# Gated products taken one block at a time instead of two joined, with a new order of all steps

## The chip, the cores and the metric

One core of one Trainium2 chip runs the whole program. The metric is the device time of one execution in microseconds. The engines that matter are TensorE (PE in the profile, its weight loads PEld), VectorE (DVE), ScalarE (ACT), GpSimd (POOL) and SyncE (SP), which here only issues transfers. Each engine takes its instructions strictly in the order in which the program lists them, so a step that waits holds everything behind it on the same engine.

## What is computed

The input `A_u` is 2048 tokens of 512 channels in bf16. It is normalized per token, and the output is the sum of the input, a long convolution and a gated layer:

```python
x = A_u
xn = _layernorm(x, axis=-1)
# A: per channel d a kernel K[d, l] = Re sum_n C * exp(dt*A*l) * dt*B, convolved causally
#    over 2048 tokens (by FFT in the reference), plus xn * Dskip
# B:
g = jnp.einsum("bsd,df->bsf", xn, w_gate)     # 512 -> 1792
u = jnp.einsum("bsd,df->bsf", xn, w_up)
h = _sigmoid(g) * u
b = jnp.einsum("bsf,fd->bsd", h, w_down)      # 1792 -> 512
return x + A(xn) + b
```

## The kernel before

**The planner.** The kernel first builds a list of steps (`pl.add`), which are numbered in the order in which they are added, each with an engine and a function that emits one or a few instructions. A hand-kept list `ORDER` of these numbers then says in which order the functions are called, and so the order of each engine's queue. Slots of buffers are handed out and given back along this list. Steps 0 to 605 are the normalization and the convolution, the steps from 606 on the gated layer; the numbers up to 605 mean the same in both kernels.

**The head.** Four loads bring tokens 0 to 511, one a part of the parameters (`l_pa`, three 128x512 blocks). TensorE first runs matmuls on zeros (`keep_warm`, L519). Tokens are normalized in pairs of tiles: VectorE and ScalarE take statistics (L542, L534), GpSimd a power (L492), VectorE scales (L554), TensorE transposes (L565), and the result goes to `xnT`: the first pair by step 35 on ScalarE (L572), the second by step 46 on VectorE (L574). Only then can the first gate matmuls run, for blocks 6 to 9 in halves (`HALF`): the first 256 tokens need step 35, the others step 46. Beside this the first parameters are worked up: step 47 an exponential on ScalarE (L608, waits for `l_pa`), steps 48 and 49 products on VectorE (L610), step 50 on ScalarE (L615, waits for 48), step 51 on VectorE (L618, L619, waits for 50), step 52 an exponential on ScalarE (L621, waits for 49).

**The convolution.** VectorE builds power tables for four chunks of 128 channels (`PCH`, chunks 0 to 3) by complex products (L736, L737, L741, L742) and squares (L795, L796, squares on ScalarE at L790), after a ladder of squarings (L669, L676, L678). When a chunk's tables are done, TensorE multiplies them (L821), ScalarE copies the result up (`kq_sb`), SyncE stores it to DRAM and loads it back transposed after every second chunk, and VectorE adds one row (L842). The last table step of chunk 3 is number 364. Then, for two halves of the channels (p = 0, 1) and eight units u each: forward transform (L883), copy up, a swap of half rows (by four transfers, or by four copies on VectorE, L896), kernel transform (L909), two products on VectorE (L914, L918), inverse transform (L933), copy up, store. p = 1 can start its L909 only after L842 of the second pair of chunks.

**The gated layer.** Tokens go in four groups of 512 (`grp`), the hidden dimension in 14 blocks of 128 (`k`), of which two neighbours make a pair `u2` that shares a slot of `hT_sb`. Per block: four gate matmuls (L1043), a sigmoid on ScalarE from PSUM into `hT_sb` (L1055, or L1058 for two blocks at once in four pairs of `JOINT`), four up matmuls (L1067), and the gated product on VectorE. For blocks in `UEV` ScalarE copies the up product from PSUM to `us_sb` first (L1082), and gives the PSUM bank back; these products are made for both blocks of a pair at once (L1087, 1024 columns). `us_sb` has two slots of two blocks. For the others VectorE reads PSUM (L1092, 512 columns). After all 14 blocks follow four down products of 14 matmuls (L1121), a copy to `glu_sb` and, for groups 0 to 2, transfers from the GpSimd queue that add the input (L1158). The last sums (L1018, L1141) and the stores end the program.

**GpSimd's other part.** For tokens 512 on, in groups of four tiles, GpSimd makes the step between statistics and scaling (L481, L482); VectorE's L501 and L502 (one step, numbers 102, 119 and 136 for the three groups) wait for it.

Of the kernel before, what the change touches and what calls it, by code (L numbers as in the profile page):

```python
# [10 lines left out]
BF = mybir.dt.bfloat16  # L11
F32 = mybir.dt.float32
I32 = mybir.dt.int32
ACT = mybir.ActivationFunctionType
ALU = mybir.AluOpType
# [10 lines left out]
FT = 14  # L26
# [21 lines left out]
FLIP = ((0, 3), (0, 5), (1, 0), (1, 1), (1, 2), (1, 4), (1, 5), (1, 6), (2, 0), (2, 4), (3, 2))  # L48
JOINT = ((0, 2), (0, 3), (0, 5), (0, 6))
PF1 = 58.63  # L50
PSIG = 18.15
# [4 lines left out]
PPROD = 23.23  # L56
# [126 lines left out]
def _consts():  # L183
# [19 lines left out]
UEV = (6, 7, 10, 11, 12, 13, 14, 15, 16, 17, 18, 19, 22, 23, 24, 25, 26, 27, 28, 29, 30, 31, 32, 33, 34, 35, 36, 37, 38, 39, 40, 41, 44, 45, 46, 47, 52, 53, 54, 55,)  # L203
# [115 lines left out]
def kernel(  # L319
# [25 lines left out]
    def bank(slot, r=0):  # L345
        if slot.pool == "s":
            return pairs[slot.idx][:, 512 * r:512 * r + 512]
        return banks[slot.idx][:]
# [17 lines left out]
    us_sb = const.tile([128, 2, 2, 512], BF, name="us_sb")  # L366
# [381 lines left out]
    for c in range(4):  # L748
# [11 lines left out]
        n = 1  # L760
# [262 lines left out]
    for grp in range(4):  # L1023
# [5 lines left out]
        for u2 in range(7):  # L1029
# [4 lines left out]
            for k in (2 * u2, 2 * u2 + 1):  # L1034
# [38 lines left out]
                un = FT * grp + k  # L1073
                on = un in UEV

                if on:
                    if k % 2 == 0:
                        eu0, es0 = (b, mu, k), es_
                        continue
                    eus, us = [], _Slot("us")  # L1080
                    for n, (sl, m_, kk) in enumerate([(b, mu, k), eu0] if (grp, u2) in FLIP else [eu0, (b, mu, k)]):
                        eus.append(pl.add("ACT", 0.48, lambda sl=sl, us=us, kk=kk: S.activation(out=us_sb[:, us.idx, kk % 2, :], in_=bank(sl), func=ACT.Identity),  # L1082
                                          [m_] + eus, PSIG, acq=[] if n else [us], rel=[sl], alt=(FT * grp + kk, 1)))

                    def fpd2(hs=hs, us=us):
                        hh = hT_sb[:, hs.idx, :, :].rearrange("p k n -> p (k n)")
                        V.tensor_tensor(out=hh, in0=hh, in1=us_sb[:, us.idx, :, :].rearrange("p k n -> p (k n)"), op=ALU.mult)  # L1087
                    prods.append(pl.add("DVE", 0.33, fpd2, [es0, es_] + eus, PPROD, rel=[us], alt=(un, 2)))
                    continue

                def fpd(sl=b, h=h):
                    V.tensor_tensor(out=h(), in0=h(), in1=bank(sl), op=ALU.mult)  # L1092
                tail = dict(rel=[b], alt=(un, 2))
                if joint and k % 2 == 0:
                    held = fpd, [mu], tail
                    continue
                if joint:
                    prods.append(pl.add("DVE", 0.33, held[0], held[1] + [es_], PPROD, **held[2]))
                prods.append(pl.add("DVE", 0.33, fpd, [es_, mu], PPROD, **tail))
        ges = []  # L1100
        for jj in range(4):
            i = grp * 4 + jj
            DP = 80 + grp + 0.5 + jj * 0.01
            late = grp in LATE
            if jj == 0:
# [105 lines left out]
```

## Time and profile before

| | |
|---|---|
| three runs | 215.75 us median (214.8 to 215.97) |
| the profiled execution | 215.17 us |
| its span, first to last instruction | 213.4 us |
| mean granted TensorE clock | 0.996 |
| moved by DMA | 42.61 MB, mean 200 GB/s |
| sigmoids L1055 / L1058 | 48 of 616 ns / 4 of 1043 ns |
| copies to `us_sb` L1082 | 40 of 621 ns |
| products that read PSUM, L1092 | 16 of 679 ns |

The span is 1.77 us shorter than the profiled execution's own time; the rest lies before the first and after the last instruction. In timeline rows the first number is the start, the second the duration from the span's start in us; instructions of one engine overlap a little, so the cost of one in a full queue is the distance between starts, not its duration.

### The profile page before, as it was taken

Reading aid. Unit: us, or ns where it says so; the run is one execution under the profiler, and the core shown is the slowest. Engines: PE = TensorE matmul, PEld = TensorE weight load, DVE = VectorE, ACT = ScalarE, POOL = GpSimd, SP = SyncE. Lnnn points to the kernel's source line nnn. Section 1 sums busy time; section 2 is a strip of 40 time slices with the busy share of each in tenths; the row PEclk is TensorE's granted clock in tenths of the full one; section 3 lists DMA queues with packets and bytes.
Section 4 is the critical chain, followed back from the end, with each engine's and each line's share of the span. In section 5 each row is a group of like instructions: output and inputs, shape, how many; then the busy total and the mean of one; then the engine's idle time right before and its main releaser. Section 6 shows DMA issues by size and latency. Waiting matters only on the chain.

```text
span 213.4 us, 4894 instructions
## 1 busy us (share of the span) xinstructions
PE 204.0 (96%) x1839; PEld 103.1 (48%) x1864; DVE 191.2 (90%) x406; ACT 176.7 (83%) x284; POOL 24.9 (12%) x40
## 2 busy tenths in 40 slices
PE   7989999999999999999999999999999999999992
PEld 2554444444444444445446465444554646634472
DVE  4799999998999999999999999999986799991493
ACT  4799999999999999988999998979899797891000
POOL 2120003009340000200000002010170200000000
PEclk9999999999999999999999999999999999999998
DMA  5999399136162243693895659768968989888944
GB/s 138 334 383 378 132 219 315 57 102 147 49 129 71 98 128 122 194 252 117 237 262 153 186 137 289 182 154 214 258 175 209 248 277 322 218 257 224 268 178 172
DMA packets 52346, 42.61 MB, mean 200 GB/s; under 512 B 16610, under 2 KB 44515, under 8 KB 52323
## 3 DMA queue, kind: packets, MB, share of 16 engines
q1 hardware_dynamic: 51154, 40.40, 64.8%
q0 software_dynamic: 864, 1.57, 4.5%
q10 hardware_dynamic: 304, 0.33, 0.5%
q8 instruction: 14, 0.23, 0.4%
q14 instruction: 10, 0.07, 0.1%
HBM read 24.99 MB, written 12.85 MB: 177 GB/s over the span
## 4 chain that ended last, share of the span: by engine, by line
DVE 55%; PE 28%; issue 5%; POOL 5%; DMA 4%; ACT 1%; DVEq 0%; ACTq 0%; SPq 0%
PE bank L1121 10%; PE bank L1043 7%; DVE big L737 6%; DVE big L736 5%; DVE stats L542 4%; DVE big L914 4%; PE bank L1067 4%; DVE big L742 3%; PE pair L909 3%; DVE hT_sb L1087 3%; DVE big L741 3%; DVE hT_sb L1092 3%; DVE big L896 3%; DVE big L678 3%; DMA big<-big 3%
## 5 line engine op out<-in xcount | busy, mean ns | idle before, releaser
L288 ACT ACTIVATE big<-pair 128x1024 bf16<-128x1024 f32 x64 | 64.6, 1041 | 5.5 <-PE pair L909 1.9
L1067 PE MATMUL bank<-xnT,wu_sb 128*128 128x512 bf16 x213 | 52.0, 380 | 1.3 <-issue 0.6
L1121 PE MATMUL bank<-wd_sb,hT_sb 128*128 128x512 bf16 (+1 forms) x231 | 50.6, 367 | 0.5 <-issue 0.2
L1043 PE MATMUL bank<-xnT,wg_sb 128*128 128x512 bf16 (+1 forms) x193 | 45.8, 371 | 0.8 <-ACT xnT L572 0.3
L1043 PEld LDWEIGHTS <-wg_sb 128*128 128x128 bf16 x240 | 22.6, 98 | 25.0 <-issue 2.7
L1121 PEld LDWEIGHTS <-hT_sb 128*128 128x128 bf16 x238 | 22.3, 98 | 25.2 <-issue 2.3
L1067 PEld LDWEIGHTS <-wu_sb 128*128 128x128 bf16 x224 | 21.0, 98 | 26.3 <-issue 3.9
L1055 ACT ACTIVATE hT_sb<-bank 128x512 bf16<-128x512 f32 x48 | 27.4, 616 | 0.1
L736 DVE TENSOR_TENSOR big<-big 128x1024 bf16<-128x1024 bf16 (+4 forms) x40 | 26.8, 670 | 0.2
L737 DVE TENSOR_TENSOR big<-big 128x1024 bf16<-128x1024 bf16 (+4 forms) x40 | 26.6, 664 | 0.0
L1082 ACT ACTIVATE us_sb<-bank 128x512 bf16<-128x512 f32 x40 | 24.0, 621 | 1.0 <-DVE hT_sb L1087 0.8
L914 DVE TENSOR_TENSOR big<-big 128x2048 bf16<-128x2048 bf16 x16 | 19.5, 1219 | 1.3 <-ACT big L288 1.3
L909 PE MATMUL pair<-big 128*128 128x256 bf16 x160 | 19.6, 273 | 0.4 <-DVE big L842 0.2
L909 PEld LDWEIGHTS <-big 128*128 128x128 bf16 x160 | 15.4, 98 | 5.3 <-issue 1.1
L741 DVE TENSOR_TENSOR big<-big 128x512 bf16<-128x512 bf16 (+4 forms) x40 | 16.6, 415 | 0.2
L742 DVE TENSOR_TENSOR big<-big 128x512 bf16<-128x512 bf16 (+4 forms) x40 | 16.6, 414 | 0.0
L790 ACT ACTIVATE sq_sb<-big 128x256 bf16<-128x256 bf16 (+2 forms) x20 | 13.4, 668 | 1.8 <-DVE big L742 1.6
L933 PE MATMUL pair<-big 64*64 64x512 bf16 (+1 forms) x256 | 13.3, 328 | 0.3 <-ACT big L288 0.2
L1087 DVE TENSOR_TENSOR hT_sb<-hT_sb,us_sb 128x1024 bf16<-128x1024 bf16 x20 | 13.5, 683 | 0.0
L288 ACT ACTIVATE big<-big 128x256 bf16<-128x256 bf16 x30 | 13.4, 450 | 0.0
L542 DVE BATCH_NORM_STATS2 stats<-big 128x6 f32<-128x512 bf16 x15 | 9.7, 681 | 3.0 <-DMA big<-in_A_u_dram 3.0
L669 ACT ACTIVATE big<-big 128x1024 f32<-128x1024 f32 x11 | 11.9, 1083 | 0.0
(100 smaller groups left out, 228.9 us busy)
## 6 DMA issues: line engine op xcount, KB each, us to landing
big<-c_E SPq DMA_DIRECT2D x13, 320.0 KB, 4.2
z_scr<-big SPq DMA_DIRECT2D x16, 256.0 KB, 4.8
big<-z_scr SPq DMA_DIRECT2D x16, 256.0 KB, 4.1
v_scr<-big SPq DMA_DIRECT2D x16, 256.0 KB, 3.9
big<-big SPq DMA_DIRECT2D x44, 64.0 KB, 3.3
big<-in_A_u_dram SPq DMA_DIRECT2D x4, 512.0 KB, 10.3
wu_sb<-in_B_w_up_dram SPq DMA_DIRECT2D x2, 896.0 KB, 9.7
wd_sb<-in_B_w_down_dram SPq DMA_DIRECT2D x1, 1792.0 KB, 9.8
```

What stands on the lines that cost most here:

```text
L288: nc.scalar.activation(out=get(out), in_=get(in_), func=ACT.Identity)
L736: V.tensor_tensor(out=wide(outp), in0=wide(lo), in1=mre, op=ALU.mult)
L737: V.tensor_tensor(out=wide(tb()), in0=wide(lo), in1=mim, op=ALU.mult)
L741: V.tensor_tensor(out=outp[:, :, 0], in0=outp[:, :, 0], in1=tb()[:, :, 1], op=opr)
L742: V.tensor_tensor(out=outp[:, :, 1], in0=outp[:, :, 1], in1=tb()[:, :, 0], op=opi)
L909: T.matmul(two(sk)[:, o:o + DW], es()[:, g, kt, :], kTv[p][:, :, kt, :], start=kt in (0, NKT - 1), stop=kt >= NKT - 2)
L914: V.tensor_tensor(out=pp().rearrange("p q h m -> p (q h) m"), in0=xx().rearrange("p q h m -> p (q h) m"), in1=kb()[:, 0:2 * DW].unsqueeze( ...
L1043: T.matmul(bank(sl, k % 2)[:, c0:c1], w[:, kt, k * 128:(k + 1) * 128], xnT[:, grp, kt, c0:c1], start=(kt == 0), stop=(kt == KT - 1))
L1055: S.activation(out=hT_sb[:, hs.idx, k % 2, :], in_=bank(sl), func=ACT.Sigmoid)
L1067: T.matmul(bank(sl), wu_sb[:, kt, k * 128:(k + 1) * 128], xnT[:, grp, kt, :], start=(kt == 0), stop=(kt == KT - 1))
L1082: eus.append(pl.add("ACT", 0.48, lambda sl=sl, us=us, kk=kk: S.activation(out=us_sb[:, us.idx, kk % 2, :], in_=bank(sl), func=ACT.Identity ...
L1121: T.matmul(bank(po)[:, 0:c[1] - c[0]], hT_sb[:, hts[k // 2].idx, k % 2, jj * 128:(jj + 1) * 128], wd_sb[:, k, c[0]:c[1]], start=first and ...
```

## The change

The joined product and its list `FLIP` go. Every block in `UEV` has its own copy and its own product of 512 columns; `us_sb` has two slots of one block each. Every block has a step for the copy (one that emits nothing where the block isn't in `UEV`), which gives 966 steps in place of 930. `UEV` names 40 blocks as before, but others: 7, 11, 14 and 8 in groups 0 to 3, against 6, 12, 14 and 8. `ORDER` is new as a whole; its first 21 entries, up to the scaling of the first two tiles (steps 32 and 33), are the same. The scratch that holds the descriptors of transfers issued by GpSimd goes from 8192 bytes to the library's default. No matmul, sigmoid, table step or transfer is added or removed.

```diff
-FLIP = ((0, 3), (0, 5), (1, 0), (1, 1), (1, 2), (1, 4), (1, 5), (1, 6), (2, 0), (2, 4), (3, 2))
-UEV = (6, 7, 10, 11, 12, 13, 14, 15, 16, 17, 18, 19, 22, 23, 24, 25, 26, 27, 28, 29, 30, 31, 32, 33, 34, 35, 36, 37, 38, 39, 40, 41, 44, 45, 46, 47, 52, 53, 54, 55,)
+UEV = (0, 6, 7, 9, 11, 12, 13, 14, 15, 16, 17, 18, 19, 21, 23, 24, 25, 26, 28, 29, 30, 31, 32, 33, 34, 35, 36, 37, 38, 39, 40, 41, 43, 44, 46, 47, 49, 52, 54, 55,)
 ORDER = [
-    0, 1, 2, 3, 5, 4, 12, 11, 24, 26, 25, 27, 28, 30, 29, 36, 37, 38, 31, 32, 33, 39, 41, 40, 47, 20, 34, 42, 43, 44,
-    48, 35, 21, 22, 23, 639, 50, 49, 51, 52, 45, 46, 98, 7, 629, 632, 644, 92, 96, 94, 630, 53, 606, 99, 93, 607, 6,
...
-    868, 852, 447, 350, 870, 819, 421, 514, 905, 364, 365, 572, 515, 367, 366, 876, 853, 587, 433, 368, 877, 499, 516,
...
+    0, 1, 2, 3, 5, 4, 12, 11, 24, 26, 25, 27, 28, 30, 29, 36, 37, 38, 31, 32, 33, 14, 39, 41, 40, 47, 20, 34, 48, 6,
+    49, 50, 42, 51, 52, 7, 43, 44, 35, 21, 98, 22, 92, 23, 635, 45, 646, 46, 94, 639, 96, 53, 652, 636, 95, 647, 93,
...
+    432, 333, 560, 364, 426, 940, 513, 392, 902, 446, 433, 886, 514, 447, 365, 887, 366, 367, 845, 442, 765, 368, 926,
...
-    us_sb = const.tile([128, 2, 2, 512], BF, name="us_sb")
+    us_sb = const.tile([128, 2, 512], BF, name="us_sb")
...
+                us = _Slot("us")
                 on = un in UEV

-                if on:
-                    if k % 2 == 0:
-                        eu0, es0 = (b, mu, k), es_
-                        continue
-                    eus, us = [], _Slot("us")
-                    for n, (sl, m_, kk) in enumerate([(b, mu, k), eu0] if (grp, u2) in FLIP else [eu0, (b, mu, k)]):
-                        eus.append(pl.add("ACT", 0.48, lambda sl=sl, us=us, kk=kk: S.activation(out=us_sb[:, us.idx, kk % 2, :], in_=bank(sl), func=ACT.Identity),
-                                          [m_] + eus, PSIG, acq=[] if n else [us], rel=[sl], alt=(FT * grp + kk, 1)))
-
-                    def fpd2(hs=hs, us=us):
-                        hh = hT_sb[:, hs.idx, :, :].rearrange("p k n -> p (k n)")
-                        V.tensor_tensor(out=hh, in0=hh, in1=us_sb[:, us.idx, :, :].rearrange("p k n -> p (k n)"), op=ALU.mult)
-                    prods.append(pl.add("DVE", 0.33, fpd2, [es0, es_] + eus, PPROD, rel=[us], alt=(un, 2)))
-                    continue
+                def feu(sl=b, us=us, on=on):
+                    if on:
+                        S.activation(out=us_sb[:, us.idx, :], in_=bank(sl), func=ACT.Identity)
+                eu = pl.add("ACT", 0.48, feu, [mu], PSIG, acq=[us] if on else [], rel=[b] if on else [], alt=(un, 1))

-                def fpd(sl=b, h=h):
-                    V.tensor_tensor(out=h(), in0=h(), in1=bank(sl), op=ALU.mult)
-                tail = dict(rel=[b], alt=(un, 2))
+                def fpd(sl=b, h=h, us=us, on=on):
+                    V.tensor_tensor(out=h(), in0=h(), in1=us_sb[:, us.idx, :] if on else bank(sl), op=ALU.mult)
+                tail = dict(rel=[us] if on else [b], alt=(un, 2))
...
-    nc = _bacc.Bacc("TRN2", target_bir_lowering=False, num_devices=1, dynamic_dma_scratch_size=8192)
+    nc = _bacc.Bacc("TRN2", target_bir_lowering=False, num_devices=1)
```

More of the change, by code (lines that the diff above doesn't have):

```diff
@@ L1073 @@
                 un = FT * grp + k
+                us = _Slot("us")
                 on = un in UEV
-                if on:
-                    if k % 2 == 0:
-                        eu0, es0 = (b, mu, k), es_
-                        continue
-                    eus, us = [], _Slot("us")
-                    for n, (sl, m_, kk) in enumerate([(b, mu, k), eu0] if (grp, u2) in FLIP else [eu0, (b, mu, k)]):
-                        eus.append(pl.add("ACT", 0.48, lambda sl=sl, us=us, kk=kk: S.activation(out=us_sb[:, us.idx, kk % 2, :], in_=bank(sl), func=ACT.Identity),
-                                          [m_] + eus, PSIG, acq=[] if n else [us], rel=[sl], alt=(FT * grp + kk, 1)))
-                    def fpd2(hs=hs, us=us):
-                        hh = hT_sb[:, hs.idx, :, :].rearrange("p k n -> p (k n)")
-                        V.tensor_tensor(out=hh, in0=hh, in1=us_sb[:, us.idx, :, :].rearrange("p k n -> p (k n)"), op=ALU.mult)
-                    prods.append(pl.add("DVE", 0.33, fpd2, [es0, es_] + eus, PPROD, rel=[us], alt=(un, 2)))
-                    continue
-                def fpd(sl=b, h=h):
-                    V.tensor_tensor(out=h(), in0=h(), in1=bank(sl), op=ALU.mult)
-                tail = dict(rel=[b], alt=(un, 2))
+                def feu(sl=b, us=us, on=on):
[5 more added lines that the diff above has]
+                tail = dict(rel=[us] if on else [b], alt=(un, 2))
                 if joint and k % 2 == 0:
-                    held = fpd, [mu], tail
+                    held = fpd, [eu, mu], tail
                     continue
@@ L1098 @@
                     prods.append(pl.add("DVE", 0.33, held[0], held[1] + [es_], PPROD, **held[2]))
-                prods.append(pl.add("DVE", 0.33, fpd, [es_, mu], PPROD, **tail))
+                prods.append(pl.add("DVE", 0.33, fpd, [es_, eu, mu], PPROD, **tail))
         ges = []
```

76 rows, old and new, of the table ORDER are left out of this document.

## The prediction

> **What bounds the kernel now.** I read the page's totals first, then the busy time by stage, then what TensorE and VectorE waited for.
>
> ```profile
> span 213.4 us, 4894 instructions
> PE 204.0 (96%) x1839; PEld 103.1 (48%) x1864; DVE 191.2 (90%) x406; ACT 176.7 (83%) x284; POOL 24.9 (12%) x40
> ```
>
> ```profile
> 20.00:80.00 60.00, 58.98 (x397) 25.98 (x405) 58.65 (x140) 59.20 (x99) 10.97 (x14) 1.00 0.48 138
> 80.00:155.00 75.00, 74.21 (x774) 37.60 (x773) 74.45 (x163) 68.54 (x118) 4.53 (x11) 1.00 0.75 198
> 155.00:192.00 37.00, 35.60 (x462) 19.78 (x468) 32.23 (x56) 32.83 (x42) 5.22 (x3) 1.00 0.86 243
> 192.00:213.40 21.40, 17.50 (x141) 10.35 (x139) 10.13 (x12) 0.59 (x1) 0.00 (x0) 0.96 0.71 210
> ```
>
> ```profile
> PE pair L821 <- DVE big L286: 0.4, 1, 0.4
> PE pair L909 <- DVE big L842: 0.2, 1, 0.2
> ```
>
> ```profile
> DVE big L896 <- issue: 2.8, 1, 2.8
> DVE big L914 <- ACT big L288: 1.3, 1, 1.3
> DVE ln_ri_f L501 <- POOL ln_sd_b L482: 1.2, 1, 1.2
> ```
>
> The columns of the second fence are stretch, length, then busy time of PE, PEld, DVE, ACT, POOL, clock, DMA. From 20 to 192 us TensorE stands still for 1.02 + 0.79 + 1.40 = 3.2 us, and its longest wait there is 0.4 us. So its queue sets the time: no matmul goes away, hence between 20 and 192 us no order can win more than 3.2 us, and each microsecond for which TensorE lacks work is lost. VectorE is as full until 155 us (58.65 of 60, 74.45 of 75), ScalarE until 80. VectorE's longest wait, 2.8 us at L896, lies after 155 us.
>
> The place where both meet is chunk 3's tables:
>
> ```profile
> 154.49 0.44 DVE L742 TENSOR_TENSOR big<-big 128x512 bf16<-128x512 bf16 x1
> 154.83 0.68 DVE L1092 TENSOR_TENSOR hT_sb<-hT_sb,bank 128x512 bf16<-128x512 bf16 x1
> ...
> 154.92 1.47 PE L821 MATMUL pair<-big 128*32 128x82 bf16 x128
> ```
>
> The last table step ends at 154.49 + 0.44 = 154.93 us and L821 starts at 154.92 without an idle mark: VectorE delivers just when TensorE asks. From the two step lists I counted what stands ahead of step 364 and of chunk 3's L821. On TensorE the same gate and up matmuls (91 blocks), down products and units, in both kernels; on VectorE the same table and normalization steps, and 42 blocks' products. So whichever of the two reaches this point later in the new kernel shifts everything behind it.
>
> **The products.**
>
> ```profile
> L1087 DVE TENSOR_TENSOR hT_sb<-hT_sb,us_sb 128x1024 bf16<-128x1024 bf16 x20 | 13.5, 683 | 0.0
> L742 DVE TENSOR_TENSOR big<-big 128x512 bf16<-128x512 bf16 x16 | 6.9, 430 | 0.0
> ...
> 118.56 0.67 DVE L1087 TENSOR_TENSOR hT_sb<-hT_sb,us_sb 128x1024 bf16<-128x1024 bf16 x1
> 119.16 0.67 DVE L736 TENSOR_TENSOR big<-big 128x1024 bf16<-128x1024 bf16 x1
> ```
>
> A joined product costs 119.16 - 118.56 = 0.60 us of the queue. No product of 512 bf16 columns from SBUF to SBUF is there; the same operation at L742 on the same shape costs 154.83 - 154.49 = 0.34 us. Two of them cost 0.68, so 0.08 us more a pair. Of the 20 pairs 16 stand ahead of step 364 (groups 0 to 2; in the new list 32 single ones, and 10 that read PSUM in both): 16 x 0.08 = 1.3 us, with nothing beside it to hide it, VectorE being full. The upper bound takes the whole 0.43 us duration: 32 x 0.43 - 16 x 0.60 = 4.2 us. A gain is excluded, as columns and operation are the same. The other four pairs come after 155 us, where VectorE idles 37.00 - 32.23 = 4.8 us, and cost nothing; without that idle time 0.3 us. The copies L1082 stay 40 on ScalarE.
>
> **The head.** The new list puts steps 48 and 49 (which need the parameters) ahead of the scaling of tiles 2 and 3 on VectorE, and steps 50 and 52 ahead of step 35, the copy of the first `xnT`, on ScalarE.
>
> ```profile
> 7.11 0.63 ACT L608 ACTIVATE big<-big 128x512 bf16<-128x512 bf16 x1 [0.72 <-DMA big<-in_A_par_dram]
> 7.64 1.00 ACT L572 ACTIVATE xnT<-pair 128x1024 bf16<-128x1024 bf16 x1
> 9.06 0.72 ACT L615 ACTIVATE big<-big,magic 128x512 f32<-128x512 f32 x1 [0.41 <-DVE big L610]
> 9.69 0.61 ACT L621 ACTIVATE big<-big 128x512 f32<-128x512 f32 x1
> ```
>
> ```profile
> 7.62 0.74 DVE L554 TENSOR_SCALAR big<-big,ln_m_f,ln_ri_f 128x512 bf16<-128x512 bf16 x2
> 8.27 1.29 DVE L610 TENSOR_TENSOR big<-big 128x512 f32<-128x512 bf16 x2
> 9.81 0.43 DVE L618 TENSOR_SCALAR big<-big 128x512 f32<-128x512 f32 x1 [0.25 <-ACT big L615]
> 10.28 0.69 DVE L619 SCALAR_TENSOR_TENSOR big<-big 128x512 f32<-128x512 f32 x1
> 10.89 0.68 DVE L574 COPY xnT<-pair 128x1024 bf16<-128x1024 bf16 x1
> 11.49 2.46 DVE L542 BATCH_NORM_STATS2 stats<-big 128x6 f32<-128x512 bf16 x4
> ```
>
> ```profile
> 1.43 5.30 PE L519 MATMUL bank<-glu_sb 128*128 128x512 bf16 x12 [1.43 <-POOL rz L513]
> ...
> 7.15 1.24 PE L519 MATMUL bank<-glu_sb 128*128 128x512 bf16 x5
> 8.70 0.61 PE L1043 MATMUL bank<-xnT,wg_sb 128*128 128x256 bf16 x4 [0.30 <-ACT xnT L572]
> ...
> 11.62 0.60 PE L1043 MATMUL pair<-xnT,wg_sb 128*128 128x256 bf16 x4 [0.56 <-DVE xnT L574]
> ```
>
> The parameters set the pace: L608 ends at 7.74. Then step 48 at 7.81; L615 comes 9.06 - 8.27 = 0.79 later, at 8.60; L621 0.63 later, at 9.23; step 35 some 0.54 later, at 9.77, and it takes 1.00. The first gate matmuls start at about 10.8, not 8.70. On VectorE: 48 and 49 until 9.0; L618 at about 9.35, L619 0.47 later, the two scalings 0.61 later, at 10.43, until 11.1; then two statistics that the new list puts first (0.60 each), and step 46 at 12.3, until 13.0. TensorE's second halves start at 13.0 for 11.62: **1.4 us later**, at the same point of its queue, with no slack behind. If the parameters came 0.72 us sooner (all of L608's wait), 0.7; if none of the first gates' 10.83 - 8.70 is caught up, 2.1. VectorE is only 0.2 us late, since the two statistics are done earlier than before: 12.88 against 11.49 + 2 x 0.60 = 12.69.
>
> **GpSimd's step for the normalization.**
>
> ```profile
> 33.62 0.57 POOL L481 TENSOR_SCALAR ln_ve_b<-mvb 128x4 bf16<-128x4 bf16 x1 [17.31 <-DVE mvb L543]
> ...
> 48.35 4.17 POOL L481 TENSOR_SCALAR ln_ve_b<-mvb 128x4 bf16<-128x4 bf16 x1 [13.04 <-DVE mvb L543]
> 52.60 1.04 POOL L482 TENSOR_TENSOR ln_sd_b<-ln_ve_b,half 128x4 bf16<-128x4 bf16 x1
> ```
>
> The same L481 took 0.57 us once and 4.17 us once, the second time under back-to-back bf16 products of VectorE and until VectorE itself stood waiting for it (the 1.2 us at L501). In the new list the second group's L501 has only four steps behind its last statistics (a table product, L676 and L678, two gated products, some 2.7 us; before, fourteen), so a second such wait is possible: 0 to 1.7 us (0.57 + 1.04 + start); I take 0.7, the third group's wait staying at 1.2 (0 to 1.7). [...]
>
> **The rest.** The load of tokens 1536 to 2047 is now behind the store of group 1's rows on SP and may make VectorE wait at most about 1.5 us; I take 0: the store waits for tiles 4 to 7, which I estimate at 22 us by adding up VectorE's queue, the first use at 32 us by the same sum. The load of the last transform's table goes from SP's place 115 to 150, before the last stores; what covers it is TensorE's two down products ahead of its use, and without them its whole landing would count. Transfers from GpSimd:
>
> ```profile
> L1158 POOL DMA_DIRECT2D glu_sb<-in_A_u_dram x4 | 3.7, 994 | 30.5 <-ACT glu_sb L288 30.3 <-ACT big L288 0.2
> ...
> ACT us_sb L1082 <- DVE hT_sb L1087: 0.8, 1, 0.8
> ```
>
> Whatever the larger scratch does to these 1 us issues, GpSimd is 12% busy and their data is wanted only after 192 us: 0. With one block a slot, a third copy waits for the first product, and behind it stand ScalarE's other copies, whose PSUM TensorE wants. Before, that happened once, 0.8 us, after 155 us. I take 0; bound below.
>
> **Sum.** At chunk 3's tables VectorE is late by 1.3 + 0.2 + 0.7 = 2.2 us, TensorE by 1.4 less its 0.4 wait at L821. The later one counts: 2.2. Behind it
>
> ```profile
> 161.81 3.44 DVE L896 COPY big<-big 32x1024 bf16<-32x1024 bf16 x8 [2.83 <-issue]
> 165.28 0.28 DVE L842 TENSOR_TENSOR big<-big,dskr 1x256 bf16<-1x256 bf16 x1
> ```
>
> L842 now stands between the two groups of four copies, and the 0.2 us that L909 waited for it may go: -0.2. Total +2.0: span 215.4, the profiled execution 215.17 + 2.0 = 217.2. That execution lies 0.58 below the median of the runs, so **217.7 us** by the median.
>
> **Rivals.**
> (a) No measurable change, +0.3 us, 216.1: the parameters come early, GpSimd slips in, and VectorE's old 1.2 us wait at L501 goes; then 1.3 + 0.2 - 1.2 at VectorE, and TensorE's late start is taken out of its pauses. For it: the 0.57 us row. Against: TensorE's pauses are many and short.
> (b) The copy buffer starves ScalarE, +4.6: of the 18 copies of groups 0 and 1, each waits half a 0.60 us step, 5.4 us, less ScalarE's idle 60.00 - 59.20 = 0.8; 220.3. For it: ScalarE is full until 80 us. Against: the one wait seen.
> (c) TensorE falls back to half rate in its new pause from 7.15 + 1.24 = 8.4 to 10.8 us. The first twelve matmuls of 512 columns took 5.30 us, 0.44 each, the five at 7.15 0.25 each; another such run-in loses about half of 5.30, so +2.0 + 2.6 = +4.6, 220.3. Against: a pause of 2.4 us is short beside the run-in. [...]
> (d) Faster: the closing stage tightens, because the copy-up that L896 waited 2.8 us for comes earlier, and TensorE's pauses go entirely: 1.4 - 3.2 = -1.8, 213.9. It decides once all pauses together fall below 0.7 us (1.4 - 3.2 + 0.7 = -1.1). Against: the pauses sit everywhere, 1.8 of 3.2 ahead of 155 us.
>
> **The numbers.** The forecast 0.58, (a) 0.16, (b) 0.12, (c) 0.07, (d) 0.07. A measurement of this kernel tells 0.5%, 1.1 us, from no change. The forecast's own range is 216.2 to 219.2; some 0.06 of it falls below +1.1. Slower 0.71, same 0.22, faster 0.07. The range of 8 in 10 runs from 215.7 (into (a)) to 220.4 ((b) and (c) at the end).
>
> **What would show it.** First gate matmul near 10.8 us and second halves near 13.0; L1087's successor at about 0.34 us a start; L501 waiting twice; L821 of chunk 3 at 156.5 to 157.5 with an idle mark on VectorE. Wrong, if TensorE's pauses between 20 and 192 us stay at 3.2 us and L821 of chunk 3 starts before 156; or if ScalarE's waits for gated products pass 2 us.

## The result, and the profile after

The changed kernel takes 217.23 us (median of 20 runs, 215.36 to 218.65), the kernel before 215.48 us on the same chip (20 runs, 214.8 to 216.99): 1.0065 times as long, 95% interval 1.0048 to 1.0083. The forecast was 217.7, with 215.7 to 220.4 as its range.

The profiled execution of the changed kernel happens to be the fastest of the 20, 215.36 us, so its total is not typical. First its totals and its busy time by stage (stretch, length, then PE, PEld, DVE, ACT, POOL, clock, DMA):

```profile
span 213.4 us, 4950 instructions
PE 204.7 (96%) x1864; PEld 102.5 (48%) x1864; DVE 192.4 (90%) x426; ACT 177.1 (83%) x284; POOL 16.3 (8%) x40
```

```profile
20.00:80.00 60.00, 60.00 (x436) 26.84 (x435) 59.45 (x149) 59.92 (x101) 7.13 (x16) 1.00 0.50 138
80.00:155.00 75.00, 74.92 (x734) 37.16 (x732) 74.58 (x169) 68.08 (x117) 4.17 (x8) 1.00 0.73 196
155.00:192.00 37.00, 36.22 (x469) 19.56 (x468) 32.74 (x60) 33.13 (x42) 1.07 (x3) 1.00 0.88 244
```

TensorE's pauses between 20 and 192 us are 0.08 + 0.78 = 0.86 us here, against the 3.2 that the prediction read from the profile of before. The two numbers can't be compared: this profile has a record of every matmul (1864 beside 1864 weight loads), the one of before has 1839 beside 1864, and a matmul without a record looks like a pause. The experiment e2 below has a fair value. Then the places of the forecast, from the timeline of the same execution:

```profile
10.49 0.60 PE L1044 MATMUL pair<-xnT,wg_sb 128*128 128x256 bf16 x4 [2.48 <-ACT xnT L573]
12.68 0.60 PE L1044 MATMUL pair<-xnT,wg_sb 128*128 128x256 bf16 x4
...
25.91 0.42 DVE L1084 TENSOR_TENSOR hT_sb<-hT_sb,us_sb 128x512 bf16<-128x512 bf16 x1
26.25 0.69 DVE L677 SCALAR_TENSOR_TENSOR big<-big 128x512 f32<-128x512 f32 x1
...
28.78 0.23 POOL L482 TENSOR_SCALAR ln_ve_b<-mvb 128x4 bf16<-128x4 bf16 x1 [12.93 <-DVE mvb L544]
...
155.03 1.42 PE L822 MATMUL pair<-big 128*32 128x82 bf16 x128
...
165.51 0.28 DVE L843 TENSOR_TENSOR big<-big,dskr 1x256 bf16<-1x256 bf16 x1 [0.24 <-DMA big<-k_scr]
165.84 2.36 PE L910 MATMUL pair<-big 128*128 128x256 bf16 x20 [0.39 <-DVE big L843]
```

The first gates and the second halves start late, nearly as forecast (10.8 and 13.0). A single product costs the queue 26.25 - 25.91 = 0.34 us, as forecast. But GpSimd's step for the second group takes 0.23 us and nobody waits for it, and chunk 3's tables start at 155.03, 0.11 later than before, not 2. Behind them a wait stands that the forecast did not have: the row addition waits for the reload of `k_scr`. Most executions are over a microsecond longer than this one, so the first experiment was to take a more typical one.

### The profile page after: what moved, and what is told of

Same layout as the page of the kernel before. It is cut to its first block, busy times and chain, and to the rows that moved or that the text cites. A ratio compares the mean times of both kernels' runs of the same rounds, so it can differ in the third digit from the quotient of the medians.

```text
span 213.4 us, 4950 instructions
## 1 busy us (share of the span) xinstructions
PE 204.7 (96%) x1864; PEld 102.5 (48%) x1864; DVE 192.4 (90%) x426; ACT 177.1 (83%) x284; POOL 16.3 (8%) x40
## 4 chain that ended last, share of the span: by engine, by line
PE 79%; DMA 7%; ACT 7%; DVE 3%; SPq 1%; issue 1%; DVEq 0%; ACTq 0%
PE bank L1113 22%; PE bank L1068 20%; PE bank L1044 15%; PE pair L910 9%; PE pair L934 5%; PE pair L1044 3%; DMA big<-k_scr 2%; ACT big L289 2%; PE pair L822 2%; DVE big L1019 2%; DMA big<-in_A_par_dram 2%; DMA big<-big 2%; ACT kq_sb L289 1%; DMA k_scr<-kq_sb 1%; PE pair L696 1%; SPq L423 1%
## 5 line engine op out<-in xcount | busy, mean ns | idle before, releaser
L1068 PE MATMUL bank<-xnT,wu_sb 128*128 128x512 bf16 x224 | 54.0, 380 | 0.0
L1044 PE MATMUL bank<-xnT,wg_sb 128*128 128x512 bf16 (+1 forms) x200 | 47.8, 371 | 0.0
L1056 ACT ACTIVATE hT_sb<-bank 128x512 bf16<-128x512 f32 x48 | 28.3, 611 | 1.0 <-PE bank L1044 0.6
L1080 ACT ACTIVATE us_sb<-bank 128x512 bf16<-128x512 f32 x40 | 24.7, 627 | 0.2 <-PE bank L1068 0.2
L1084 DVE TENSOR_TENSOR hT_sb<-hT_sb,us_sb 128x512 bf16<-128x512 bf16 x40 | 16.4, 415 | 2.8 <-ACT us_sb L1080 2.7
L289 ACT ACTIVATE big<-big 128x256 bf16<-128x256 bf16 x30 | 12.7, 449 | 0.0
```

The lines of the kernel that those rows point to most:

```text
L289: nc.scalar.activation(out=get(out), in_=get(in_), func=ACT.Identity)
L1044: T.matmul(bank(sl, k % 2)[:, c0:c1], w[:, kt, k * 128:(k + 1) * 128], xnT[:, grp, kt, c0:c1], start=(kt == 0), stop=(kt == KT - 1))
L1056: S.activation(out=hT_sb[:, hs.idx, k % 2, :], in_=bank(sl), func=ACT.Sigmoid)
L1068: T.matmul(bank(sl), wu_sb[:, kt, k * 128:(k + 1) * 128], xnT[:, grp, kt, :], start=(kt == 0), stop=(kt == KT - 1))
L1080: S.activation(out=us_sb[:, us.idx, :], in_=bank(sl), func=ACT.Identity)
```

## The experiments

All were timed against the kernel before on the same chip. In c1, g1, g2, r1, r2, b1 and r3 the line numbers are 8 higher. The table has, from each profile, the start of chunk 3's tables on TensorE (L821 of before, L822 of after), the start of the row addition behind the reload (L842, L843), the distance between the two (the round trip through DRAM), what is left of the span after the row addition, and the ratio of the timed runs. The profiles of r1 and r2 fell on executions in which TensorE's clock fell (means of 0.992 and 0.990).

| kernel | tables | row addition | round trip | rest | ratio (95%) |
|---|---|---|---|---|---|
| before | 154.92 | 165.28 | 10.36 | 48.1 | |
| after, first profile | 155.03 | 165.51 | 10.48 | 47.9 | 1.0065 (1.0048 to 1.0083) |
| e0, the same kernel | 155.59 | 166.67 | 11.08 | 47.8 | 1.0077 (1.0048 to 1.0106) |
| e1 | 155.69 | 167.13 | 11.44 | 47.9 | 1.0051 (1.0025 to 1.0076) |
| e2 | 154.93 | 165.30 | 10.37 | 48.1 | 1.0057 (1.003 to 1.0084) |
| e3 | 155.90 | 166.46 | 10.56 | 48.1 | 1.004 (1.002 to 1.0061) |
| w1 | 155.36 | 166.39 | 11.03 | 48.3 | 1.0064 (1.004 to 1.0088) |
| c1 | 155.70 | 166.82 | 11.12 | 47.9 | 1.0084 (1.0052 to 1.0117) |
| g1 | 154.53 | 165.15 | 10.62 | 48.1 | 1.0001 (0.9974 to 1.0028) |
| g2 | 155.32 | 166.56 | 11.24 | 47.9 | 1.0059 (1.0032 to 1.0086) |
| r1 | 156.54 | 167.22 | 10.68 | 47.9 | 1.0035 (1.0007 to 1.0063) |
| r2 | 154.65 | 167.78 | 13.13 | 49.7 | 1.0107 (1.0049 to 1.0166) |
| b1 | 154.75 | 164.32 | 9.57 | 49.8 | 1.0019 (0.9999 to 1.0039) |
| r3 | 155.58 | 166.89 | 11.31 | 49.0 | 1.0032 (1.0008 to 1.0055) |

**e0: the changed kernel once more.**

> The changed kernel unchanged, timed beside the kernel before on one chip, and a second profile of it: its one profile so far has a span of 213.4 us and was the fastest of its 20 executions (215.36 us against a median of 217.23). Theory H (the head sets the loss): the second profile, at about 215 us of span, shows TensorE's first gate matmuls later still than in the first profile (10.5 us), by about the difference of the spans. Theory V (VectorE's 20 more instructions set it): the head is as in the first profile and TensorE stands waiting for VectorE between 20 and 160 us instead. Time by both: 1.005 to 1.009 of the kernel before.

216.9 us (median of 6). The timeline of its profile:

```profile
48.09 6.68 POOL L482 TENSOR_SCALAR ln_ve_b<-mvb 128x4 bf16<-128x4 bf16 x1 [16.55 <-DVE mvb L544]
...
55.92 0.18 DVE L502 RECIPROCAL ln_ri_f<-ln_sd_b 128x4 f32<-128x4 bf16 x1 [1.24 <-POOL ln_sd_b L483]
...
155.59 1.42 PE L822 MATMUL pair<-big 128*32 128x82 bf16 x128
...
166.67 0.28 DVE L843 TENSOR_TENSOR big<-big,dskr 1x256 bf16<-1x256 bf16 x1 [0.85 <-DMA big<-k_scr]
167.00 2.36 PE L910 MATMUL pair<-big 128*128 128x256 bf16 x20 [1.00 <-DVE big L843]
```

Here the third group's GpSimd step is held for 6.68 us and VectorE waits 1.24 us. In the first profile the same step took 0.58 us behind the same instructions of VectorE. So the wait at L502 can come in one execution and not in another. Neither theory is borne out: the first gates start at 10.08 us, 0.41 earlier than in the first profile, and TensorE's longest wait between 20 and 192 us is the 1.00 us for the row addition. The ledger of this execution against the one of before: tables + 0.67, round trip + 0.72, rest - 0.29, together the 1.1 us by which the span is longer (214.5 for 213.4). This execution too is the fastest of its set, 0.3 us below the median of the six.

**e1 and e2: the head alone.** e1 is the changed kernel with the old order of the head, e2 the kernel before with the new one.

```diff
 e1 (after)
-    ..., 47, 20, 34, 48, 6,
-    49, 50, 42, 51, 52, 7, 43, 44, 35, 21, 98, 22, 92, 23, 635, ...
+    ..., 47, 20, 34, 42, 43, 44, 48, 35, 6,
+    50, 49, 51, 52, 7, 21, 22, 23, 635, 45, 646, 46, 98, 92, 94, ...
 e2 (before)
-    ..., 47, 20, 34, 42, 43, 44,
-    48, 35, 21, 22, 23, 639, 50, 49, 51, 52, 45, 46, 98, 7, ...
+    ..., 47, 20, 34, 48, 49, 50, 42,
+    51, 52, 43, 44, 35, 21, 98, 22, 92, 23, 639, 45, 46, 7, ...
```

> The changed kernel with the head's order of the kernel before: the scaling of tiles 2 and 3 (steps 42 to 44) and the copy of the first xnT (step 35) again ahead of the parameters' steps 48 to 52, and step 46 ahead of two statistics; nothing else moved. Theory H: first gate matmuls at about 8.7 us, second halves at about 11.6, and 1.1 to 1.8 us less than the changed kernel: 0.998 to 1.002 of the kernel before. Theory V: the head hides behind VectorE's tables, so the time stays at 1.005 to 1.009.

> The kernel before with the head's order of the changed one (steps 48, 49, 50, 52 ahead of 42 and 35, two statistics ahead of 46), its joined products and the rest of its order kept. Theory H: first gate matmuls near 10.6 us, and 1.1 to 1.8 us more: 1.005 to 1.008. Theory V: at most 0.2 us, the lateness of VectorE in the head: 1.000 to 1.002.

e1: 216.55 us (8 runs), e2: 216.66 us (12 runs). The timeline of e2:

```profile
10.12 0.60 PE L1043 MATMUL bank<-xnT,wg_sb 128*128 128x256 bf16 x4 [2.10 <-ACT xnT L572]
...
12.42 0.60 PE L1043 MATMUL pair<-xnT,wg_sb 128*128 128x256 bf16 x4
...
79.04 1.42 PE L821 MATMUL pair<-big 128*32 128x82 bf16 x128 [0.34 <-DVE big L286]
...
154.93 1.48 PE L821 MATMUL pair<-big 128*32 128x82 bf16 x128
```

The gates start 1.42 us late and the second halves 0.80, yet chunk 0's tables start at 79.04 and chunk 3's at 154.93, 0.00 and 0.01 us from before: TensorE has caught up by then, as it waits for VectorE at chunk 0's tables, 0.34 us here and 0.4 before.

This profile has all 1864 matmuls, so it also tells what TensorE's pauses are in the old order. Its stages, with columns as above:

```profile
20.00:80.00 60.00, 59.63 (x406) 26.26 (x408) 58.49 (x139) 59.54 (x100) 10.65 (x14) 1.00 0.48 139
80.00:155.00 75.00, 75.00 (x782) 37.54 (x769) 74.45 (x163) 68.51 (x118) 4.52 (x10) 1.00 0.73 197
155.00:192.00 37.00, 36.35 (x468) 19.80 (x468) 32.23 (x56) 32.85 (x42) 5.23 (x3) 1.00 0.85 243
```

They are 0.37 + 0.00 + 0.65 = 1.02 us, not 3.2, at the same span of 213.4 us. In e0 the same three stages have 0.43 + 0.05 + 1.38 = 1.86 us.

By its time e1 agrees with theory V and e2 with theory H, which can't both hold. The granted clock accounts for it. The profiled execution of e2 took 215.58 us. But of e2's 12 runs five have a mean granted clock of 0.992 and take 217.54 us on average, and the other seven, at 0.996 to 1.0, take 215.95 (median 215.88, for 215.5 before). The changed kernel's own 20 runs have six at 0.992. Neither e1 (8 runs) nor e3 (12) has one. This is what w1, c1 and r1 look at.

**e3: the products alone**, the kernel before with each joined product issued as two:

```diff
-                        hh = hT_sb[:, hs.idx, :, :].rearrange("p k n -> p (k n)")
-                        V.tensor_tensor(out=hh, in0=hh, in1=us_sb[:, us.idx, :, :].rearrange("p k n -> p (k n)"), op=ALU.mult)
+                        for kk in range(2):
+                            hh = hT_sb[:, hs.idx, kk, :]
+                            V.tensor_tensor(out=hh, in0=hh, in1=us_sb[:, us.idx, kk, :], op=ALU.mult)
```

> The kernel before with each joined product issued as two instructions of 512 columns at the same place, order and buffers kept. Theory V: 0.08 us a pair on a full VectorE, 16 pairs ahead of chunk 3's tables, so L821 of chunk 3 starts 1.3 us later and the time is 1.005 to 1.007. Theory H: it is taken up by VectorE's waits (1.2 us at L501, 2.8 us after 158 us): 0.999 to 1.003.

216.42 us (12 runs), 1.004, between the two theories. From its timeline:

```profile
119.36 0.74 DVE L1088 TENSOR_TENSOR hT_sb<-hT_sb,us_sb 128x512 bf16<-128x512 bf16 x2
120.03 0.68 DVE L736 TENSOR_TENSOR big<-big 128x1024 bf16<-128x1024 bf16 x1
...
155.90 1.61 PE L821 MATMUL pair<-big 128*32 128x82 bf16 x128
```

Two single products cost 120.03 - 119.36 = 0.67 us of the queue for 0.60 joined. Sixteen such pairs make 1.1 us, and the tables start 0.98 later. This is the one term that was seen to act just where it was placed.

**w1 and c1: TensorE's pause ahead of the first gates.** w1 is the changed kernel with eight more matmuls on zeros in that pause, c1 has the five that stand there moved ahead of the transposes, which makes the pause longer.

```diff
 w1
-        keep_warm(3 if n < 3 else 1, -9 + n)
+        keep_warm({0: 3, 5: 1, 6: 9}[n], -9 + n)
 c1
-    ..., 47, 20, 34, ..., 35, 21, 98, 22, 92, 23, 635, ...
+    ..., 47, 20, 21, 22, 23, 34, ..., 35, 98, 92, 635, ...
```

> The changed kernel with eight more matmuls on zeros (512 columns, 0.22 us each) behind the five at 6.8 us, so that TensorE's pause ahead of the first gate matmuls shrinks from 1.6 to 2.5 us to under 0.8 us; the first gates stay near 10.1 to 10.6 us. Theory 1 (in about a third of the executions the pause lets TensorE's clock fall to half for some 3.4 us, which costs 1.5 to 1.7 us): no execution with a mean clock of 0.992; the median falls by 0.3 to 0.7 us, ratio 1.003 to 1.005, and the executions above 217.5 go. Theory 2 (the start being late costs, whatever the clock; the 0.992 belongs to the machine and not to the pause): ratio 1.006 to 1.008 as before, and 0.992 still comes in a third of the executions.

> The changed kernel with the five matmuls on zeros moved ahead of the first transposes: the same work, but the pause ahead of the first gate matmuls grows to about 3 us. Theory 1 (the longer the pause, the more executions lose the clock): a mean clock of 0.992 or less in most executions, the profile shows the gate matmuls of 256 columns some 0.22 us apart instead of 0.11 for about 3.4 us, ratio 1.010 to 1.013 (217.6 to 218.3 us). [...]

w1: 216.81 us (12 runs), none at 0.992. c1: 216.96 us (12 runs), two at 0.992 (218.38 and 217.74). So the pause has to do with the clock, as theory 1 of w1 says, but the median does not fall when it is filled, though the same theory forecast that. Theory 1 of c1 is wrong: with the longer pause two of 12 executions lose the clock, not most. The timeline and the stages of c1:

```profile
10.30 0.60 PE L1052 MATMUL pair<-xnT,wg_sb 128*128 128x256 bf16 x4 [2.85 <-ACT xnT L581]
```

```profile
12.00:16.00 4.00, 4.00 (x31) 2.81 (x30) 3.84 (x11) 3.88 (x8) 1.57 (x2) 1.00 1.08 366
```

Here the gates run at full rate after a pause of 2.85 us: the granted clock is 1.00, and four matmuls of 256 columns take 0.44 us by their starts.

**g1 and g2: GpSimd's step.** VectorE's step 136 (L501, L502 in the kernel before) is moved behind a later product that reads PSUM, its two scalings 137 and 138 further behind; g1 is the kernel before, g2 the changed one.

```diff
 g1
-    ..., 672, 136, 189, ..., 144, 137, 138, 697, ...
+    ..., 705, 136, 85, ..., 709, 137, 138, 221, ...
 g2
-    ..., 83, 136, 700, ..., 125, 137, 162, ..., 754, 138, 146, ...
+    ..., 755, 136, 705, ..., 720, 137, 138, 171, ...
```

> The kernel before, with VectorE's step that waits for GpSimd in the third group (L501, L502) moved behind the next product that reads PSUM (66 us), and its two scalings behind the one at 73 us; nothing else. Theory 1 (the 1.2 us for which VectorE stood at 53.7 lie on the chain to the tables; GpSimd gets in during a product that reads PSUM): no wait at L501, chunk 0's tables at 77.8 instead of 79.0, chunk 3's at 153.7, ratio 0.994 to 0.997 (214.2 to 215.0 us). Theory 2 (GpSimd is held until VectorE has nothing to issue): L501 waits 1.2 us again at its new place, chunk tables and time unchanged, ratio 1.000. Theory 3 (TensorE's queue sets the time, and its pauses only move): no wait at L501, tables earlier, but ratio 0.999 to 1.001.

> The changed kernel with the same move (L502, L503 behind the product that reads PSUM at 63 us, the two scalings behind the one at 71 us). Theory 1 (this wait comes in most executions of the changed kernel, 1.2 us, and was missing in its first profile by chance): no wait at L502, chunk 3's tables near 154.5, median 0.5 to 1.0 us lower, ratio 1.002 to 1.004. Theory 2 (the wait isn't on the path, as the chain has room in the new order): ratio 1.006 to 1.008 as without the move.

In neither does VectorE wait for GpSimd at this step any more. g1's tables start 0.39 us earlier, not 1.2, and its time stays (215.44 us, 12 runs); g2's median is 216.89 (12 runs, one of them 221.64), as without the move. Theory 1 of both falls, theory 3 of g1 and theory 2 of g2 hold. How GpSimd came through, in the timeline of g2:

```profile
48.23 12.86 POOL L490 TENSOR_SCALAR ln_ve_b<-mvb 128x4 bf16<-128x4 bf16 x1 [16.57 <-DVE mvb L552]
61.18 1.11 POOL L491 TENSOR_TENSOR ln_sd_b<-ln_ve_b,half 128x4 bf16<-128x4 bf16 x1
...
60.61 0.77 DVE L670 CAST big<-big 128x512 bf16<-128x512 f32 x2
62.41 0.36 DVE L804 TENSOR_TENSOR big<-sq_sb 128x384 bf16<-128x384 bf16 x1 [1.02 <-ACT sq_sb L799]
```

An instruction that took 0.23 to 0.59 us for the first two groups of tokens was held for 12.86 us, under more than 25 instructions of VectorE, until just before VectorE stood waiting for ScalarE (from 60.61 + 0.77 = 61.38). In g1 the same one took 1.21 us, the next 1.85, with VectorE busy throughout and no product that reads PSUM among its instructions from 48.26 to 51.41 us. So it got in there without such a product; that GpSimd gets in during one, as theory 1 of g1 supposed, is not shown.

**r1, r2, b1, r3: the round trip.** Every profile so far ends 47.8 to 48.3 us behind the row addition, so what differs from kernel to kernel lies ahead of it: the tables and the round trip. In the new order GpSimd issues the accumulations of tiles 10, 11 and 6, 7 together, just ahead of the round trip. The DMA queues' packets between 155.5 and 161 us, in e0:

```profile
q1 hardware_dynamic: 1732, 0.62, 47.4%
q0 software_dynamic: 176, 0.31, 34.0%
...
k_scr<-kq_sb SPq DMA_DIRECT2D x2, 96.0 KB, 3.0
```

and in the kernel before, where these accumulations went out at 131 and 150 us:

```profile
q1 hardware_dynamic: 2049, 0.76, 55.7%
...
q0 software_dynamic: 2, 0.00, 0.2%
...
k_scr<-kq_sb SPq DMA_DIRECT2D x2, 96.0 KB, 2.6
```

r1 takes them apart in the changed kernel, r2 puts them beside the round trip in the kernel before, b1 shortens the round trip there (with g1's move), and r3 is r1 with w1's matmuls.

```diff
 r1
-    ..., 367, 845, 442, 765, 368, ...
+    ..., 760, 765, 347, ..., 373, 845, 895, ...
 r2
-    ..., 811, 746, 414, ..., 870, 819, 421, ...
+    ..., 376, 819, 746, 448, ...
 b1 (beside the move of g1)
-    ..., 871, 536, 449, 371, 562, ..., 501, 372, 893, ...
+    ..., 449, 371, 536, 562, 563, 372, 892, ...
 r3 (beside the move of r1)
-        keep_warm(3 if n < 3 else 1, -9 + n)
+        keep_warm({0: 3, 5: 1, 6: 9}[n], -9 + n)
```

> The changed kernel with the two accumulations that GpSimd issues together at 151.5 and 152.0 us (tokens of tiles 10, 11 and of 6, 7) taken apart: the one for 6, 7 right behind that of 4, 5 (130 us), the one for 10, 11 behind L843 of the second pair. Theory 1 (their packets, 25 to 40% of the DMA engines in 155.5 to 161 us, stretch the round trip of chunk 3's table rows through DRAM, and the end hangs 48 us behind L843): no GpSimd packets in that window, L843 10.4 to 10.7 us behind chunk 3's L822 instead of 11.0 to 11.4, ratio 1.002 to 1.005. Theory 2 (the round trip is the queue's own latency): L843 still 11 us behind, ratio 1.006 to 1.008.

> The kernel before with the accumulations for tiles 6, 7 and 10, 11 (there at 131 and 150 us) both behind GpSimd's memset at 155 us, so that they run beside the round trip of chunk 3's table rows; nothing else. Theory 1: chunk 3's L821 stays at 154.9, L842 moves from 165.3 to 165.8 to 166.6 and waits for the transfer from k_scr, the end by the same amount: ratio 1.002 to 1.006. Theory 2: L842 at 165.3 to 165.5, ratio 0.999 to 1.001.

> The kernel before with three moves: VectorE's step that waits for GpSimd later (as in g1), the load from z_scr for unit 5 (256 KB) behind the reload of k_scr on SP, and the row addition L842 ahead of the second four row copies L896. Theory 1 (the end hangs on chunk 3's tables plus the round trip): chunk 3's L821 at 154.5, L842 on the reload's arrival at 164.2 to 164.8 instead of 165.3, the end 0.5 to 1.0 us earlier, ratio 0.995 to 0.998. Theory 2 (other chains set the end as well): L842 earlier, but ratio 0.999 to 1.001; slower if the load from z_scr is now late for its unit.

> The changed kernel with the two accumulations taken apart (as in r1) and with the eight more matmuls on zeros in TensorE's pause (as in w1). Theory 1 (r1's executions with a mean clock of 0.992 lost it in that pause, about 1.7 us each, and what is left are the single products, worth 0.9 to 1.0 us): no execution at 0.992, gates at full rate from the first, L843 10.4 to 10.7 us behind chunk 3's L822, ratio 1.001 to 1.004 and no execution over 217.5 us. Theory 2 (the falling clock has another cause): some executions at 0.992, ratio as in r1 or above, 1.003 to 1.006.

r2: 219.41 us (6 runs). With GpSimd's packets at 59.5% of the engines the stores land twice as late (5.7 us for 2.6 in the kernel before), the tables being on time. The DMA view of 155.5 to 161 us, then the timeline:

```profile
q0 software_dynamic: 263, 0.49, 59.5%
...
k_scr<-kq_sb SPq DMA_DIRECT2D x2, 96.0 KB, 5.7
```

```profile
167.78 0.28 DVE L850 TENSOR_TENSOR big<-big,dskr 1x256 bf16<-1x256 bf16 x1 [2.77 <-DMA big<-k_scr]
...
168.11 3.84 PE L917 MATMUL pair<-big 128*128 128x256 bf16 x20 [2.96 <-DVE big L850]
```

So accumulations beside the round trip do stretch it, here by 2.8 us, more than theory 1 had. The 219.41 us hold more than that: in four of the six executions the mean clock is 0.984 to 0.990; the other two took 216.8 us, 1.2 above before. In the changed kernel taking the accumulations away is worth less: r1 has 1.0035 for 1.0065, r3 1.0032 for w1's 1.0064. Both pairs show 0.3%, but their intervals overlap. r1's round trip of 10.68 us is as theory 1 has it, r3's is 11.31 us with none of GpSimd's packets in it (the reload alone took 5.6 us). The rest of the round trip's scatter stays open. r3's theory 1 also forecast no execution over 217.5 us, yet two are over it, one of them the profiled one (217.96); TensorE waits 1.0 us for a transfer from `v_scr` in its last part, which is 49.0 us long.

b1: 216.13 us (12 runs). The row addition comes at 164.32, 0.96 earlier than before, and the end is no earlier: 49.8 us follow. So the 48 us hold only as long as the row addition is what comes last. The timeline of b1, its wait, and the timeline of the kernel before show what takes over:

```profile
164.32 0.28 DVE L850 TENSOR_TENSOR big<-big,dskr 1x256 bf16<-1x256 bf16 x1 [0.96 <-DMA big<-k_scr]
164.63 1.71 DVE L904 COPY big<-big 32x1024 bf16<-32x1024 bf16 x4
166.38 1.29 DVE L1095 TENSOR_TENSOR hT_sb<-hT_sb,us_sb 128x1024 bf16<-128x1024 bf16 x2
```

```profile
ACT us_sb L1090 <- DVE hT_sb L1095: 1.9, 1, 1.9
```

```profile
165.49 1.27 DVE L1087 TENSOR_TENSOR hT_sb<-hT_sb,us_sb 128x1024 bf16<-128x1024 bf16 x2
```

The row addition now stands ahead of four copies and two gated products, and holds them while it waits 0.96 us for the reload. The first product starts at 166.38 for 165.49, and ScalarE waits 1.9 us for it in place of 0.8. What a shorter round trip is worth without that price was not tried. No version beat the kernel before.

r1's profile fell on an execution at 0.992 (217.19 us) and shows what it is. Its timeline and stages:

```profile
10.49 0.62 PE L1052 MATMUL pair<-xnT,wg_sb 128*128 128x256 bf16 x4 [2.05 <-ACT xnT L581]
...
11.76 1.06 PE L1052 MATMUL bank<-xnT,wg_sb 128*128 128x256 bf16 x4
12.61 1.06 PE L1052 MATMUL pair<-xnT,wg_sb 128*128 128x256 bf16 x4
...
156.54 1.42 PE L830 MATMUL pair<-big 128*32 128x82 bf16 x128
```

```profile
8.00:12.00 4.00, 1.95 (x17) 1.49 (x15) 3.17 (x8) 3.68 (x5) 0.00 (x0) 0.87 1.00 355
12.00:16.00 4.00, 3.95 (x23) 2.84 (x23) 4.00 (x12) 3.88 (x6) 1.01 (x2) 0.71 1.09 366
```

Four gate matmuls take 12.61 - 11.76 = 0.85 us instead of the 0.44 of c1: half rate. By the two stages the clock is missing 4 x 0.13 + 4 x 0.29 = 1.7 us, so at half rate it ran for an estimated 3.4. The tables start at 156.54, about 1 us later than in the other profiles of this order. With the pause in the program (the changed kernel, e0, e2, c1, g2, r1) 20 of 74 runs are at 0.992; without it (e1, e3, w1, g1, r3, b1) none of 68. r2 is in neither group, as its clock falls at another place (last section). r3 has the pause filled, none of its 12 runs at 0.992, and yet its median, 216.47, is hardly below r1's 216.79. The falling clock thus makes some executions longer, and explains little of the changed kernel's median: without the six at 0.992 its 20 runs have 217.14 us for 217.23. In e2 it explains most of the loss (215.88 for 216.66, with 215.5 before).

## Why the prediction was right in size, and which steps failed

**The bound** (TensorE's pauses, 3.2 us, the most that an order can win) was read from an incomplete record. Of the 32 gaps between 20 and 192 us in the profile of before, 23 lie where two starts are about one matmul too far apart; they fit the matmuls without a record and make 1.8 of the 3.2 us. That leaves an estimate of 1.4 us, and e2 shows 1.02. The changed kernel has 0.86 in its first profile and 1.86 in e0, so no gain in pauses is shown out of which losses could have been paid. For the same reason half of the statement that would have proved the forecast wrong, pauses still at 3.2 us, can't be tested; its other half, tables ahead of 156, came true in both profiles of the changed kernel.

**The products**, + 1.3 us at the tables: right in mechanism, 0.98 measured (e3); a pair costs 0.07 more, not 0.08. Alone they cost the kernel before 0.4%, of the 0.65 that the whole change costs. That the tables were only 0.11 late in the first profile of the changed kernel does not speak against this: VectorE stood idle for 0.55 + 0.42 = 0.97 us between 20 and 155 us there, as L502 did not wait, and for 1.9 in the profiles of before and of e0. In e0 the tables were 0.67 late.

**The head**: the starts were forecast at 10.8 and 13.0; 10.49 and 12.68 were found in the first profile, 10.08 and 12.61 in e0. "With no slack behind" failed: e2 shows the late start gone by chunk 0's tables. It cost the sum nothing, since VectorE's side counted. What the late start brought instead is rival (c), a fall to half rate in the new pause. It was priced at 4.6 us and set aside by the author's estimate that a pause of 2.4 us is short beside the run-in of 5.30; it comes in 20 of 74 runs and took 1.7 us of clock in r1. It came with the pause of 2.05 us in r1 and not with that of 2.85 us in c1's profile. So a short pause was no protection here, and the length of the pause alone does not tell whether the clock falls.

**GpSimd's step**, + 0.7 for a second wait: failed. The second group's step went through in 0.23 us, and the third group's wait of 1.24 us, where it came, was worth 0.39 us at the tables (g1) and nothing at the end. The price of a wait was taken as its length; what it delays had room, as VectorE then waited for ScalarE (0.8 us at the gated products in g1). How long GpSimd's instruction is held was not to be read from one row: 4.17 us in the profile of before, 6.68 in e0, 12.86 in g2, there under more than 25 instructions of VectorE.

**The copy buffer and the scratch**, 0: ScalarE's waits for gated products, which were to stay below 2 us, are 0 in the first profile and 0.5 us in e0. Rival (b) falls. Neither was tried alone.

**Behind the tables**, - 0.2 at L842: failed. The forecast followed the row addition's place in VectorE's queue and not the arrival of its data. In the kernel before data and queue come almost together; in the new order the data come last in every profile, and the round trip is 0.1 to 1.1 us longer. Why it is longer is shown only in part: accumulations beside it stretch it (r2), but r3 has none beside it and is 0.95 longer.

So the forecast had 2.2 - 0.2 = 2.0 us, and e0 has 0.67 + 0.72 less 0.29 of span, 1.1: at the tables, which it named, a third of what it had there, and about as much again behind them, which it had not seen. The medians are 1.4 (e0's set) to 1.75 us (the first 20 runs) above before; no profile shows what lies between 1.1 and these. The total was right by luck, as terms that were too large stood in for ones that were missing.

## What to carry to other kernels

Where a step waits for both a queue and a transfer, follow the transfer too, from its first store to its landing, and look at what else the new order issues beside it. A wait that is seen in a profile is worth its length only if nothing behind it has room: moving it away and seeing where the next meeting point lands costs one run. Before reading a pause on TensorE, compare the number of its matmuls with that of its weight loads: here 23 missing records between 20 and 192 us looked like 1.8 us that could be won. And take a second profile before explaining the first, since here the first was the fastest of 20.

## What the runs showed of the hardware

In r2 TensorE waited 2.96 us in the middle of the program, and the 20 matmuls behind took 3.84 us instead of the 2.36 of the kernel before. From 168 to 172 us the granted clock was 0.60, so here it fell in mid-program too:

```profile
168.00:172.00 4.00, 3.89 (x21) 2.85 (x22) 2.29 (x4) 1.62 (x2) 1.19 (x1) 0.60 0.95 224
```

A small GpSimd instruction, the step for the normalization, took 0.23 (first profile of the changed kernel) to 12.86 us (g2) beside VectorE. For the third group, behind the same instructions of VectorE, it took 0.58 us in that first profile and 6.68 in e0.
